# A transformer block's attention, re-cut into 32 units with the MLP's second product woven between their steps

## Chip, cores, metric

One core of a Trainium2 chip (trn2). The metric is the device time of one execution in microseconds. Executions of a kernel were timed in rounds beside executions of the kernel before, on the same chip.

Engines: PE (TensorE matmul), PEld (its weight load), DVE (VectorE), ACT (ScalarE), POOL (GpSimd). PSUM has 8 banks; a bank holds 128 x 512 fp32. "Granted clock" is the share of full speed that PE's throttle granted in the records; 1.00 is full speed.

## The reference, cut to what matters

```python
xn = layernorm(x)                       # x: 2048 tokens x 1024
out = x + A(xn) + B(xn)
# A: 32 heads of 32, four segments of 512 tokens, causal softmax inside a segment,
#    plus a linear memory M (phi(q) @ M / phi(q) @ z) carried over the segments; o = g*a_mem + (1-g)*a_dot; o @ wo
# B: h = layernorm(xn);  u = gelu(h^T w1 + b1) over tokens (F = 3584);  y = (u w2 + b2)^T
```

All large products come to 2816 matmuls of 128 x 128 x 512 in both kernels: 896 for each MLP product, 768 for q, k, v, 256 for `wo`. Attention itself is small on PE: per group of four heads 16 score matmuls, 40 for the weighted values, and a few for the memory.

## The kernel before

Five stages stand one after the other: layernorms; the first product; the second product with segment 0's projections between its tiles; four attention segments, with projections of the next segment and output projection of the last one as filler; a tail.

```python
def group_logits(self, s, i, g, step):          # LOGIT_STEPS = [[0], [1], [2, 3]]: blocks of 128 keys
    for r in range(4):                           # four heads, PSUM bank r each
        with fw.group(reads=[RkT[g], RqT[g]], writes=[self.R_bank[lb]]):
            for kb in kbs: fw.mm(...)            # scores, 32 rows of the array
        fw.op("act", ... activation(dst, ps_u, ACT.Exp, scale=SCALE) ...)      # one exp per head and step
        for kb in kbs: fw.op("pool", ... affine_select(diag, ...) ...)         # one causal mask per head and block
# ...
# gelu: Identity+bias on ACT, two scalar_tensor_tensor on DVE, Sigmoid on ACT, product on DVE
# output projection: its own accumulation, then
fw.op("dve", lambda e: e.tensor_tensor(dst, ps_t, dst, op=ALU.add), ...)       # onto rows read back from the output
```

Every operation goes through a helper that turns reads and writes into semaphore waits. One detail of it comes back later: a group of matmuls that writes a bank also waits for the last writer of that bank, even if that is PE itself.

```python
for r in writes:
    w = r.w                     # the token of the last writer, raised when its last matmul has completed
    ...
    add(w)
```

The softmax here doesn't subtract the row's maximum and nothing guards it: scores larger than these inputs give would overflow.

Of the kernel before, what the change touches and what calls it, by code (L numbers as in the profile page):

```python
# [23 lines left out]
C_GELU = 0.7978845608028654  # L24
K_CUBE = 0.044715
LN_EPS = 1e-5
MEM_EPS = 1e-6

PT_OFF = [0, 512, 896, 1152]
# [70 lines left out]
class FW:  # L100
    N_DMA_SEMS = 64
    N_OUT_SEMS = 24
# [161 lines left out]
class _BandStream:  # L264

    def __init__(self, fw, slots, slot_res, depth, issuer="sp"):
        self.fw = fw
        self.slots = slots
        self.res = slot_res
        self.n = len(slots)  # L270
        self.depth = depth
        self.bands = []
        self.issued = 0
        self.issuer = issuer

    def add(self, src_ap, dst_fn=None):
        self.bands.append((src_ap, dst_fn))
        return len(self.bands) - 1

    def slot_of(self, b):  # L280
        return b % self.n

    def ensure(self, b):
        target = min(b + self.depth, len(self.bands) - 1)
        while self.issued <= target:
            k = self.issued
            src, dst_fn = self.bands[k]
            si = self.slot_of(k)
            dst = dst_fn(self.slots[si]) if dst_fn else self.slots[si][:]
            self.fw.dma(dst, src, writes=[self.res[si]], issuer=self.issuer)  # L290
            self.issued += 1


class _Task:
    __slots__ = ("est", "run", "band")

    def __init__(self, est, run, band=None):
        self.est = est
        self.run = run
        self.band = band  # L300


class _Filler:
    def __init__(self, bands):
        self.q = deque()
        self.bands = bands
        self.budget = 0.0

    def add(self, tasks):
        self.q.extend(tasks)  # L310

    def total(self):
        return sum(t.est for t in self.q)

    def run_one(self):
        t = self.q.popleft()
        if t.band is not None:
            b, stream = t.band
            stream.ensure(b)
        t.run()  # L320
        return t.est

    def step(self, quantum):
        self.budget += quantum
        while self.q and self.budget >= self.q[0].est * 0.5 and self.budget > 0:
            self.budget -= self.run_one()

    def drain(self):
        while self.q:
            self.run_one()  # L330
        self.budget = 0.0
# [21 lines left out]
class _Kernel:  # L353
    def __init__(self, nc, ctx, A_x, A_wq, A_wk, A_wv, A_wo, A_beta, B_w1, B_b1, B_w2, B_b2, out):
        self.nc = nc
        self.ctx = ctx
        self.A_x, self.A_wq, self.A_wk, self.A_wv, self.A_wo, self.A_beta = A_x, A_wq, A_wk, A_wv, A_wo, A_beta
        self.B_w1, self.B_b1, self.B_w2, self.B_b2, self.out = B_w1, B_b1, B_w2, B_b2, out

    def sb(self, arena, shape, dtype, side):  # L360
        self._sb_n = getattr(self, "_sb_n", 0) + 1
        name = f"sbt{self._sb_n}"
        return arena.enter_context(self.nc.sbuf_tensor(name, list(shape), dtype, side=side))

    def res(self, name, init=None):
        return Res(name, init)

    def build(self):
        nc, ctx = self.nc, self.ctx
        fw = self.fw = FW(nc, ctx)  # L370

        self.x_d = self.A_x[0].rearrange("(c p) d -> p c d", p=P)
        self.out_d = self.out[0].rearrange("(c p) d -> p c d", p=P)

        self.ps = ctx.enter_context(nc.psum_tensor("ps_all", [P, 8, 512], F32))
        self.R_bank = [Res(f"bank{b}", bank=b) for b in range(8)]

        pa = self.pa = ExitStack()
        ctx.enter_context(pa)
        L = "left"  # L380
        self.ident = self.sb(pa, [P, P], BF16, L)
        self.brow1 = self.sb(pa, [N_FCH, P], BF16, L)
        self.brow2 = self.sb(pa, [N_TCH, P], BF16, L)
        self.beta_sb = self.sb(pa, [P, N_HEAD], BF16, L)
        self.gcol = self.sb(pa, [P, N_HEAD], F32, L)
        self.gm = self.sb(pa, [P, N_HEAD], F32, L)
        self.b1c = self.sb(pa, [P, N_FCH], F32, L)
        self.b2c = self.sb(pa, [P, N_TCH], F32, L)
        self.xnT = self.sb(pa, [P, N_DCH, S_TOK], BF16, L)
        LNR = self.LNR = 4  # L390
        self.ln_st = self.sb(pa, [P, 2, LNR, 12], F32, L)
        self.ln_mv = self.sb(pa, [P, 2, LNR, 2], F32, L)
        self.ln_rs = self.sb(pa, [P, 2, LNR], F32, L)
        self.ln_nb = self.sb(pa, [P, 2, LNR], F32, L)
        self.er = self.sb(pa, [P, 2, 512], BF16, L)
        self.MZ32 = self.sb(pa, [P, 8, 33], F32, L)
        self.MZbf = [self.sb(pa, [P, 8, 132], BF16, L) for _ in range(2)]
        self.s1 = self.sb(pa, [P, 4, 16], F32, L)
        self.s2 = self.sb(pa, [P, 4, 16], F32, L)

        self.R_ident = Res("ident")
        self.R_brow1 = Res("brow1")
        self.R_brow2 = Res("brow2")
        self.R_beta = Res("beta")
        self.R_gcol = Res("gcol")
        self.R_gm = Res("gm")
        self.R_b1c = Res("b1c")
        self.R_b2c = Res("b2c")
        self.R_xnT = [Res(f"xnT{c}") for c in range(N_TCH)]
        self.R_er = [Res(f"er{i}") for i in range(2)]  # L410
        self.R_MZ32 = [Res(f"mz32_{g}") for g in range(8)]
        self.R_MZbf = [[Res(f"mzbf{i}_{g}") for g in range(8)] for i in range(2)]
        self.R_lnA = [Res(f"lnA{c}") for c in range(LNR)]
        self.R_lnB = [Res(f"lnB{c}") for c in range(LNR)]
        self.R_s1 = Res("s1")
        self.R_s2 = Res("s2")
        self.R_out = [Res(f"outc{c}") for c in range(N_TCH)]

        bl = self.bl = ExitStack()
        Rt = "right"  # L420
        self.xB = self.sb(bl, [P, N_TCH, D_MODEL], BF16, Rt)
        self.gT = self.sb(bl, [P, N_FCH, D_MODEL], BF16, Rt)
        self.w2ring = [self.sb(bl, [P, N_FCH, P], BF16, Rt) for _ in range(2)]
        self.R_xB = [Res(f"xB{c}") for c in range(N_TCH)]
        self.R_gT = [[Res(f"gT{fc}_{h2}") for h2 in range(2)] for fc in range(N_FCH)]
        self.R_w2s = [Res(f"w2s{i}") for i in range(2)]

        be = self.be = ExitStack()
        self.h = self.sb(be, [P, N_TCH, D_MODEL], BF16, L)
        self.w1ring = [self.sb(be, [P, N_TCH, 256], BF16, L) for _ in range(2)]  # L430
        self.ga = [self.sb(be, [P, 512], F32, L) for _ in range(2)]
        self.ga2 = [self.sb(be, [P, 512], F32, L) for _ in range(2)]
        self.xn_tmp = [self.sb(be, [P, D_MODEL], BF16, L) for _ in range(2)]
        self.R_h = [Res(f"h{c}") for c in range(N_TCH)]
        self.R_w1s = [Res(f"w1s{i}") for i in range(2)]
        self.R_ga = [Res(f"ga{i}") for i in range(2)]
        self.R_ga2 = [Res(f"ga2_{i}") for i in range(2)]
        self.R_xnt = [Res(f"xnt{i}") for i in range(2)]

        self.qT = [None, None]  # L440
        self.kT = [None, None]
        self.pqT = [None, None]
        self.pk = [None, None]
        self.vA = [None, None]
        self.R_qT = [None, None]
        self.R_kT = [None, None]
        self.R_pqT = [None, None]
        self.R_pk = [None, None]
        self.R_vA = [None, None]

        block = ctx.enter_context(nc.Block())

        @block.sync
        def _(sp_eng):
            self.phase_prep()
            self.phase_B1()
            snap1 = fw.snapshot()
            self.be.close()
            self.alloc_A0(snap1)
            self.phase_B2_and_proj0()  # L460
            snap2 = fw.snapshot()
            self.bl.close()
            self.alloc_A_rest(snap2)
            self.phase_A()
            fw.final_waits()

    def alloc_A0(self, snap):
        a0 = self.a0 = ExitStack()
        self.ctx.enter_context(a0)
        L = "left"  # L470
        self.qT[0] = self.sb(a0, [P, 8, SEG_L], BF16, L)
        self.kT[0] = self.sb(a0, [P, 8, SEG_L], BF16, L)
        self.pqT[0] = self.sb(a0, [P, 8, SEG_L], BF16, L)
        self.pk[0] = self.sb(a0, [P, 4, D_MODEL], BF16, L)
        self.vA[0] = self.sb(a0, [P, 4, N_HEAD, 33], BF16, L)
        self.bands = [self.sb(a0, [P, N_DCH, 512], BF16, L) for _ in range(3)]
        self.R_qT[0] = [Res(f"qT0_{g}", snap) for g in range(8)]
        self.R_kT[0] = [Res(f"kT0_{g}", snap) for g in range(8)]
        self.R_pqT[0] = [Res(f"pqT0_{g}", snap) for g in range(8)]
        self.R_pk[0] = [[Res(f"pk0_{c}_{hh}", snap) for hh in range(2)] for c in range(4)]  # L480
# [655 lines left out]
```

## Time and profile before

| stage of the trace before | us | PE busy | granted clock |
|---|---|---|---|
| layernorms, with 4 banks of early first product | 65.3 | 31.2 | 0.88 |
| first product | 182.7 | 182.7 | 1.00 |
| second product, projections of segment 0 | 247.0 | 239.3 | 0.99 |
| attention, four segments | 390.0 | 318.4 | 0.88 |
| tail (last output projection) | 23.8 | 17.7 | 0.86 |

Median 909.7 us (907.9 to 912.1, 4 runs). The table is the view of windows, one window a stage. Its columns are: the window, its length, busy us (and instructions) of each engine, the granted clock, DMA share, GB/s.

```profile
65.30:248.00 182.70, 182.69 (x849) 82.94 (x846) 112.91 (x165) 73.16 (x112) 1.63 (x2) 1.00 0.31 80
495.00:885.00 390.00, 318.40 (x3260) 161.13 (x3260) 263.87 (x683) 203.72 (x452) 158.36 (x513) 0.88 0.26 87
```

The first page's busy line and two of its strips, each slice a fortieth of the span:

```profile
PE 789.3 (87%) x5506; PEld 377.3 (42%) x5506; DVE 494.6 (54%) x1123; ACT 318.2 (35%) x645; POOL 205.7 (23%) x555
...
PE   2479999999989999999997888798886979858867
...
PEclk9969999999999999999998988989998999976978
```

PE is 87% busy, but the strip shows where it isn't: in the first three slices and from the 22nd on, and there the clock falls too. What PE waited for in attention (view of waits, PE only, 495 to 885 us; total, times, longest):

```profile
PE ps_all L186 <- DVE sbt L1073: 18.2, 8, 2.7
PE ps_all L186 <- DVE sbt L867: 17.7, 10, 3.2
PE ps_all L192 <- DVE sbt L1106: 12.3, 3, 4.2
PE ps_all L186 <- ACT sbt L1017: 11.1, 30, 2.4
```

The waits are of several kinds: casts of the results (L1073), v casts (L867), the combine (L1106), exps (L1017). Dense work runs at one matmul of 128x512 in 215.8 ns, by the chain of waits (start, length, what):

```profile
379.22 13.81 PE ps_all L186 x64
```

### The profile page before, as it was taken

The numbers are of one execution on the slowest core, as the hardware profiler recorded it, in microseconds if no ns is written. First come the engines' busy times: TensorE is split into PE (matmuls) and PEld (weight loads), VectorE is DVE, ScalarE is ACT, GpSimd is POOL, SyncE is SP. The second block draws the span as 40 slices with busy tenths as digits, with TensorE's granted clock in tenths as the row PEclk, the third lists the DMA queues.
The fourth block names the chain that finished last, engine by engine and source line by source line (L and its number), as shares of the span: only waits on it lengthen the run. The fifth ranks groups of instructions, "written<-read, shape, count | busy, mean of one in ns | idle before, by whom it ended". The sixth has DMA issues, their size and how long they took to land.

```text
span 908.8 us, 14149 instructions
## 1 busy us (share of the span) xinstructions
PE 789.3 (87%) x5506; PEld 377.3 (42%) x5506; DVE 494.6 (54%) x1123; ACT 318.2 (35%) x645; POOL 205.7 (23%) x555
## 2 busy tenths in 40 slices
PE   2479999999989999999997888798886979858867
PEld 1234444444434444444442344444443434434434
DVE  6976765666622232222210576867677676675763
ACT  3335434333310000001100545654354544546730
POOL 4660000000010000000002334432332423426730
PEclk9969999999999999999998988989998999976978
DMA  8003223224364444525344221214232132510121
GB/s 278 1 1 93 79 61 93 67 74 112 61 182 108 110 93 101 103 53 105 65 92 138 70 94 49 93 48 139 92 106 83 57 130 94 186 48 2 48 93 47
DMA packets 128699, 80.62 MB, mean 89 GB/s; under 512 B 59002, under 2 KB 120442, under 8 KB 128634
## 3 DMA queue, kind: packets, MB, share of 16 engines
q1 hardware_dynamic: 122394, 73.43, 29.6%
q10 hardware_dynamic: 6240, 6.29, 2.2%
q8 instruction: 45, 0.74, 0.3%
q14 instruction: 20, 0.16, 0.1%
HBM read 71.32 MB, written 8.39 MB: 88 GB/s over the span
## 4 chain that ended last, share of the span: by engine, by line
PE 71%; DVE 20%; ACT 4%; DMA 2%; issue 2%; POOL 0%; SPq 0%; ACTq 0%; POOLq 0%
PE ps_all L186 70%; ACT sbt L1017 2%; DVE sbt L1067 2%; DVE sbt L1073 2%; DVE sbt L1104 1%; PE ps_all L192 1%; DVE sbt L1102 1%; DVE sbt L614 1%; DMA sbt<-in_A_wq_dram 1%; DVE sbt L613 1%; DVE sbt L849 1%; DVE sbt L646 1%; DVE sbt L1106 1%; DVE sbt L867 1%; ACT sbt L812 1%
## 5 line engine op out<-in xcount | busy, mean ns | idle before, releaser
L186 PE MATMUL ps_all<-sbt 128*128 128x512 bf16 (+5 forms) x5120 | 760.7, 312 | 74.9 <-DVE sbt L1073 18.2
L186 PEld LDWEIGHTS ps_all<-sbt 128*128 128x128 bf16 (+2 forms) x5120 | 349.4, 99 | 467.0 <-issue 94.3
L1017 ACT ACTIVATE sbt<-ps_all 128x384 bf16<-128x384 f32 (+1 forms) x384 | 169.6, 541 | 160.5 <-PE ps_all L186 122.1
L1021 POOL TENSOR_SCALAR_AFFINE_SELECT sbt<-sbt 128x128 bf16<-128x128 bf16 x512 | 156.9, 333 | 221.6 <-ACT sbt L1017 216.8
L751 DVE SCALAR_TENSOR_TENSOR sbt<-ps_all,sbt 128x512 bf16<-128x512 f32 x32 | 24.0, 751 | 150.3 <-PE ps_all L186 150.3
L192 PE MATMUL ps_all<-sbt 128*128 128x128 bf16 (+1 forms) x386 | 39.8, 255 | 39.2 <-POOL sbt L640 19.3
L712 ACT ACTIVATE sbt<-sbt 128x512 f32<-128x512 f32 x56 | 35.2, 629 | 82.2 <-DVE sbt L709 82.2
L812 ACT ACTIVATE sbt<-ps_all 128x512 bf16<-128x512 f32 x32 | 19.1, 598 | 119.7 <-DVE sbt L809 116.2
L715 DVE TENSOR_TENSOR sbt<-sbt 128x512 bf16<-128x512 f32 x56 | 38.8, 693 | 38.9 <-ACT sbt L712 38.9
L847 ACT ACTIVATE sbt<-ps_all 128x512 bf16<-128x512 bf16 x32 | 19.5, 610 | 112.8 <-PE ps_all L192 112.7
L1073 DVE CAST sbt<-ps_all 128x264 bf16<-128x264 f32 x128 | 53.6, 426 | 8.2 <-PE ps_all L186 7.1
L939 POOL MEMSET sbt<- 128x4224 bf16 x1 | 3.6, 3618 | 237.6 <-DMA out_dram<-sbt 237.6
L706 DVE SCALAR_TENSOR_TENSOR sbt<-sbt 128x512 f32<-128x512 f32 x56 | 38.7, 691 | 31.1 <-ACT sbt L703 31.1
L192 PEld LDWEIGHTS ps_all<-sbt 128*128 128x128 bf16 (+1 forms) x386 | 29.6, 115 | 58.5 <-POOL sbt L640 26.6
L703 ACT ACTIVATE sbt<-ps_all,sbt 128x512 f32<-128x512 f32 x56 | 38.2, 683 | 27.9 <-PE ps_all L186 27.9
L720 POOL MEMSET sbt<- 128x4224 bf16 x1 | 3.6, 3619 | 184.8 <-DVE sbt L715 184.8
L709 DVE SCALAR_TENSOR_TENSOR sbt<-sbt 128x512 f32<-128x512 f32 x56 | 38.8, 692 | 1.9
L828 DVE CAST sbt<-ps_all 128x512 bf16<-128x512 f32 x32 | 21.9, 689 | 32.1 <-PE ps_all L186 32.1
L809 DVE CAST sbt<-ps_all 128x512 bf16<-128x512 f32 x32 | 22.0, 687 | 29.8 <-PE ps_all L186 29.8
L904 DVE TENSOR_TENSOR sbt<-ps_all,sbt 128x512 bf16<-128x512 f32 x32 | 22.0, 689 | 26.9 <-PE ps_all L186 26.9
L867 DVE CAST sbt<-ps_all 128x512 bf16<-128x512 f32 x32 | 22.1, 690 | 22.0 <-PE ps_all L186 22.0
L849 DVE SCALAR_TENSOR_TENSOR sbt<-sbt 128x512 bf16<-128x512 bf16 x32 | 22.3, 696 | 21.4 <-ACT sbt L848 21.4
(47 smaller groups left out, 305.9 us busy)
## 6 DMA issues: line engine op xcount, KB each, us to landing
sbt<-in_B_w_dram SPq DMA_DIRECT2D x14, 1024.0 KB, 5.7
sbt<-in_B_w_dram SPq DMA_DIRECT2D x16, 896.0 KB, 6.5
sbt<-in_A_wo_dram SPq DMA_DIRECT2D x8, 1024.0 KB, 5.0
sbt<-in_A_wq_dram SPq DMA_DIRECT2D x6, 1024.0 KB, 5.4
sbt<-in_A_wk_dram SPq DMA_DIRECT2D x6, 1024.0 KB, 4.9
sbt<-in_A_wv_dram SPq DMA_DIRECT2D x6, 1024.0 KB, 4.9
sbt<-in_A_x_dram SPq DMA_DIRECT2D x4, 1024.0 KB, 8.9
out_dram<-sbt SPq DMA_DIRECT2D x16, 256.0 KB, 2.8
```

The costliest lines, as they stand in the source:

```text
L186: ins = self.nc.tensor.matmul(*args, **kwargs)
L192: ins = self.nc.tensor.transpose(out, in_, ident)
L703: fw.op("act", lambda e: e.activation(ga[:], ps_t, ACT.Identity, bias=self.b1c[:, fc:fc + 1], scale=1.0), reads=[self.R_bank[b], self.R_b1 ...
L706: fw.op("dve", lambda e: e.scalar_tensor_tensor(ga2[:], ga[:], K_CUBE, ga[:], op0=ALU.mult, op1=ALU.mult), reads=[Rga], writes=[Rga2])
L709: fw.op("dve", lambda e: e.scalar_tensor_tensor(ga2[:], ga2[:], 1.0, ga[:], op0=ALU.add, op1=ALU.mult), reads=[Rga2, Rga], writes=[Rga2])
L712: fw.op("act", lambda e: e.activation(ga2[:], ga2[:], ACT.Sigmoid, scale=2.0 * C_GELU), reads=[Rga2], writes=[Rga2])
L715: fw.op("dve", lambda e: e.tensor_tensor(dst, ga[:], ga2[:], op=ALU.mult), reads=[Rga, Rga2], writes=[self.R_gT[fc][half]])
L849: fw.op("dve", lambda e: e.scalar_tensor_tensor(dstk, e_ap, 1.0, dstk, op0=ALU.min, op1=ALU.add), reads=[Re, Rpk[c][hh]], writes=[Rpk[c][hh]])
L867: fw.op("dve", lambda e: e.tensor_copy(dst, ps_t.rearrange("p (hh d) -> p hh d", hh=16)), reads=[self.R_bank[bk]], writes=[RvA[c]])
L1017: fw.op("act", lambda e: e.activation(dst, ps_u, ACT.Exp, scale=SCALE), reads=[self.R_bank[lb]], writes=wr)
L1021: fw.op("pool", lambda e: e.affine_select(diag, diag, pattern=[[1, P]], compare_op=ALU.is_ge, fill=0.0, base=0, channel_multiplier=-1), re ...
L1073: fw.op("dve", lambda e: e.tensor_copy(dst, src), reads=small["pv"] + extra_reads, writes=[self.R_ost[gi][qb]])
```

## The change

The intent is to leave PE no gap. Attention is cut into 32 units (segment x group of four heads). A unit holds its three score steps, its four weighted sums, the projections of q and k for two units ahead, a quarter of a v block, and dense filler: 28 matmuls of the second product, and from segment 1 on 8 more of the output projection, so 36. Most of the filler stands right behind each of the three score steps, the rest at the unit's end. The output projection of segments 0 to 2 continues the second product's accumulation. Exp and mask work on four heads at once. GELU is one activation. The two layernorms are done from one set of statistics (the second variance follows from the first), and three first-product blocks, not two, are accumulated during them.

```diff
-        for r in range(4):
-            with fw.group(reads=[RkT[g], RqT[g]], writes=[self.R_bank[lb]]):
...
+        with fw.group(reads=[self.R_kT[k], self.R_qT[k]], writes=self.R_bank[0:4]):
+            for kb in kbs:
+                for r in range(4): fw.mm(...)
+        fw.op("act", lambda e: e.activation(self.pT[:, :, off:off + total], self.ps[:, 0:4, 0:total],
+                                            ACT.Exp, scale=SCALE), ...)
... (unit schedule)
+        for u in range(N_UNIT):
+            n = 28 if s == 0 else 36
+            n0, n1, n2 = (10, 8, 6) if s == 0 else (11, 9, 9)
+            n3 = n - n0 - n1 - n2
+            self.logits(u, 0)
+            if u: self.combine(u - 1)
+            self.main_emit(n0)
+            self.logits(u, 1)
+            self.main_emit(n1)
+            self.logits(u, 2)
+            self.main_emit(n2)
+            self.weigh(u, 0); self.weigh(u, 1)
+            self.proj_q(u + 2, 0)
+            self.o_transpose(u - 1, 2); self.k_transpose(u + 1, 3)
+            self.weigh(u, 2)
+            self.proj_k(u + 2, 1)
+            self.weigh(u, 3)
+            self.proj_v(m, u % 4, 2)
+            self.main_emit(n3)
... (the second product, joined with the output projection)
+            if at < N_FCH:
+                w, R_w = self.w2_ring.get(2 * j + at // 14)
+                end = min(at + n, (at // 14 + 1) * 14)
+            else:
+                end = min(at + n, total)                       # total = 28 + 8 where joined
+            with fw.group(reads=reads, writes=[self.R_bank[b]]):
+                for x in range(at, end):
+                    st, sp = x == 0, x == total - 1
+                    ...                                        # w2 x gT for x < 28, then oT x wo
... (gelu)
+        fw.op("act", ... activation(self.gT[...], self.bank(b), ACT.Gelu_apprx_tanh, bias=self.b1c[:, fc:fc + 1]), ...)
... (layernorm, pairs of chunks: rs = sqrt(1/(v + eps)) and sqrt(1/((1 + eps) v + eps^2)) in one square root)
+        fw.op("dve", lambda e: e.tensor_scalar(rs[:, :, 1:2], var, 1.0 + LN_EPS, LN_EPS * LN_EPS, ...))
```

## The prediction

> **What bounds the kernel now.** TensorE (PE), with four kinds of gap. The page gives PE 87% of 908.8 us; the windows split it:
>
> - Prologue (layernorms), 0 to 65 us: PE busy 27. VectorE is the bound (13.86 of every 15 us; 3.55 us per 128 tokens).
> - MLP first product, 66 to 248: dense. The chain shows 64 matmuls of 128x512 in 13.81 us, 215.8 ns each, which agrees with the Trainium skill, "TensorE: Matmul & The Clock Gate", section "Wait — 56ns, not 53.3ns?" (215.7 warm).
> - Second product and first projections, 248 to 495: dense but for a few us (an A_wq load, 5.4, on the chain).
> - Attention, 495 to 885 = 390 us. PE busy about 318. PE's waits are on DVE and ACT: 18.2 us on the 128x264 casts, 17.7 on v casts, 12.3 on the combine, 11.1 on exp. The same page (HAM clock gate) ties a low clock to idle; the trace agrees: 1.00 in dense windows, 0.80 where PE was busy 62%.
> - Tail, 885 to 909: 24 us.
>
> **PE work stays.** 2816 matmuls of 128x512 in both. The memory update's 384 become 96 wider; 32 memory reads and 32 transposes go.
>
> **What moves.** 896 second-product matmuls go under attention; the output projection of 12 of 16 chunks joins their accumulation, so 24 DVE adds and the read-back vanish. Exps over four heads: 3 instructions a group, not 12 (604 and 510 ns now; from that slope I estimate 1.8, 1.4, 1.4 us), masks 4, not 16.
>
> **Sum, after.**
> - Prologue: DVE per pair of chunks: 4 bn_stats at 0.72, 2 aggregates at 0.24, small operations 0.8, one normalisation 0.5: 4.7 us, against 7.1. 8 pairs after a first load at 3.5, plus pipeline: dense PE from about 47. 6 banks of hidden work are then done, not 4.
> - Hidden: 50 tiles x 16 x 0.2158 = 173, to 220.
> - First v, q, k: 64 x 0.2158 = 14, plus 3 of bubble: 237.
> - Units: attention's own PE work costs 2.9 us a group where the trace is dense (751.1 to 762.8: 11.73 us hold 40 of 128x512, 8.63, and one group). Transposes 0.45. Segment 0: 52 x 0.2158 + 3.1 = 14.3. Segments 1, 2: 60 x 0.2158 + 3.4 = 16.3. Segment 3: 15.9 less missing projections. Total 115 + 262 + 113 = 490 if dense. ACT needs 7 us a unit, DVE 9, POOL 3. The slack between score steps is thin (11 matmuls = 2.4 us against an exp of 1.8 plus latencies), so I add 0.55 a unit: 508, to 745.
> - Tail: 56 matmuls, transpose, 8 DVE adds at 0.72, last store 2.8: 22, to 767.
>
> Critical path: prologue -19, two tiles -7, joint at 248 -3, attention with second product about -112 (waits filled, clock kept at 1.00).
>
> **Predicted: 767 us, 8 in 10 between 748 and 790.** Faster 0.97, same 0.02, slower 0.01.
>
> **To check.** PE busy 95% or more after the prologue; granted clock 0.98 or more in the units; units of 14.5 to 15 us in segment 0, 16.5 to 17 in 1 and 2; dense PE from 44 to 51 us; tail 20 to 24.
>
> **What would make it wrong.** Wide exps or masks slower than their slopes say; a late buffer release in each unit (banks 0 to 3 serve scores and projections), times 32; POOL and DVE delaying each other in the prologue (a 128x1 DVE multiply takes 737 ns there against 206); a late second w1 load.

## The result

758.1 us median (757.7 to 758.7, 4 runs) against 909.7. The ratio is 0.833 (95% interval 0.831 to 0.835). Here and below a ratio is the mean time of one kernel's fast runs over that of the other's fast runs of the same rounds, so not quite the ratio of the medians.

The page after, the lines that answer to those above:

```profile
PE 717.7 (95%) x5058; PEld 338.3 (45%) x5154; DVE 277.2 (37%) x617; ACT 280.4 (37%) x301; POOL 112.3 (15%) x154
...
PE   0999999999998999999999999999999999999996
...
PEclk9999999999999999999999999999999999999999
```

The strip is full from the second slice on, but for one slice of 8 tenths and the last, and the clock stays in its top tenth. By stages (windows, columns as above): norms, first product, first projections, units of segment 0, 1, 2, 3, tail:

```profile
0.00:50.90 50.90, 31.46 (x222) 17.71 (x227) 35.00 (x97) 28.38 (x35) 25.42 (x26) 1.00 0.51 145
50.90:223.75 172.85, 172.01 (x786) 78.34 (x801) 0.00 (x0) 38.54 (x57) 0.00 (x0) 1.00 0.37 94
223.75:239.70 15.95, 14.15 (x69) 6.46 (x69) 5.15 (x8) 3.76 (x5) 0.00 (x0) 1.00 0.85 241
239.70:354.00 114.30, 112.50 (x935) 54.09 (x952) 42.77 (x110) 51.30 (x49) 19.92 (x32) 1.00 0.35 74
354.00:485.00 131.00, 128.20 (x1030) 60.88 (x1049) 65.55 (x141) 54.74 (x56) 22.11 (x32) 1.00 0.37 77
485.00:616.00 131.00, 128.23 (x1010) 60.37 (x1028) 66.78 (x142) 54.25 (x55) 22.43 (x32) 1.00 0.37 77
616.00:736.00 120.00, 116.92 (x949) 54.10 (x966) 54.06 (x109) 48.87 (x44) 22.42 (x32) 1.00 0.29 61
736.00:756.90 20.90, 14.27 (x68) 6.35 (x67) 7.93 (x14) 0.60 (x1) 0.00 (x0) 0.95 0.32 114
```

| | before | after | difference | predicted |
|---|---|---|---|---|
| norms, to dense PE | 65.3 | 50.9 | -14.4 | -19 (to about 47) |
| first product after that | 182.7 | 172.9 | -9.8 | -7 |
| second product, projections, attention | 637.0 | 512.3 | -124.7 | -115 (3 joint + 112) |
| tail | 23.8 | 20.9 | -2.9 | -2 |

The windows also split the 124.7 us of the third row. PE stood idle for 79.3 of the 637.0 us before and for 12.3 of 512.3 after, 67 less; it was busy for 557.7 us before and 500.0 after, 58 less. The 58 go with the higher clock and with the small matmuls that were dropped; no run here divides them.

What PE waited for over the whole trace after, the first four entries:

```profile
PE ps_all L194 <- DMA brow_50<-in_B_b_dram: 15.2, 1, 15.2
PE ps_all L188 <- issue: 2.2, 1, 2.2
PE ps_all L188 <- PE ps_all L188: 2.2, 14, 0.2
PE ps_all L188 <- DVE pk_1733 L673: 1.7, 1, 1.7
```

Nothing of attention is left among the waits except 1.7 us at its very start, in 239 to 736 us. What remains is the load of a bias row at the start (15.2 us; in e12_norm below, where PE does not wait for it, PE's first work still comes only at 12.9 us, after the first layernorm) and an odd entry: PE waiting for PE. It lists only 14 short waits; the experiments will show that there were more.

### The profile page after: what moved, and what is told of

Read it like the earlier page. It is cut to its first block, busy times and chain, and to the rows that moved or that the text cites. A ratio compares the mean times of both kernels' runs of the same rounds, so it can differ in the third digit from the quotient of the medians.

```text
span 756.9 us, 11693 instructions
## 1 busy us (share of the span) xinstructions
PE 717.7 (95%) x5058; PEld 338.3 (45%) x5154; DVE 277.2 (37%) x617; ACT 280.4 (37%) x301; POOL 112.3 (15%) x154
## 4 chain that ended last, share of the span: by engine, by line
PE 92%; DVE 4%; issue 2%; SPq 1%; DMA 1%; ACT 0%; DVEq 0%; another core or an unknown queue 0%
PE ps_all L188 90%; PE ps_all L194 2%; DVE ln_st L575 1%; SPq L210 1%; DVE ln_st L574 1%; DMA brow_51<-in_B_b_dram 1%; DVE ln_mv L576 0%; DVE xn_tmp_76 L607 0%; DVE ln_rs L584 0%; DVE fin_8202 L966 0%; DVE fin_8203 L966 0%; ACT xn_tmp_75 L604 0%; DVE xn_tmp_74 L607 0%; DVE ln_rs L585 0%; ACT xnT_70 L622 0%
## 5 line engine op out<-in xcount | busy, mean ns | idle before, releaser
L743 ACT ACTIVATE pT<-ps_all 128x1536 bf16<-128x1536 f32 (+1 forms) x96 | 152.9, 1593 | 201.6 <-PE ps_all L188 201.6
L749 POOL TENSOR_SCALAR_AFFINE_SELECT pT<-pT 128x512 bf16<-128x512 bf16 x128 | 86.9, 691 | 599.5 <-ACT pT L743 599.5
L662 ACT ACTIVATE gT<-ps_all,b1c 128x512 bf16<-128x512 f32 x56 | 37.8, 689 | 134.5 <-PE ps_all L188 134.5
L710 DVE CAST vA_63<-ps_all 128x512 bf16<-128x512 f32 x16 | 11.1, 694 | 187.9 <-PE ps_all L188 187.7
L188 PE MATMUL ps_all<-h,w1s_79 128*128 128x512 bf16 x311 | 72.9, 385 | 2.7 <-issue 2.2
L188 PE MATMUL ps_all<-h,w1s_80 128*128 128x512 bf16 x314 | 72.4, 381 | 0.3
L188 PE MATMUL ps_all<-h,w1s_81 128*128 128x512 bf16 x251 | 55.6, 379 | 0.3
L188 PE MATMUL ps_all<-gT,w2h_671 128*128 128x512 bf16 x213 | 53.0, 380 | 2.8 <-PE ps_all L188 0.9
L188 PE MATMUL ps_all<-gT,w2h_673 128*128 128x512 bf16 x214 | 53.1, 380 | 2.6 <-PE ps_all L188 1.1
L188 PE MATMUL ps_all<-gT,w2h_670 128*128 128x512 bf16 x219 | 53.6, 381 | 0.3
L188 PE MATMUL ps_all<-gT,w2h_672 128*128 128x512 bf16 x218 | 53.3, 381 | 0.4 <-PE ps_all L188 0.2
L783 DVE CAST ost_1736<-ps_all 128x264 bf16<-128x264 f32 (+1 forms) x64 | 23.7, 391 | 79.6 <-PE ps_all L188 79.6
L783 DVE CAST ost_1737<-ps_all 128x264 bf16<-128x264 f32 (+1 forms) x64 | 23.7, 392 | 74.7 <-PE ps_all L188 74.7
L188 PEld LDWEIGHTS ps_all<-h,w1s_80 128*128 128x128 bf16 x320 | 31.5, 98 | 38.4 <-issue 1.1
L188 PEld LDWEIGHTS ps_all<-h,w1s_79 128*128 128x128 bf16 x320 | 30.9, 99 | 37.1 <-issue 3.6
L188 PEld LDWEIGHTS ps_all<-h,w1s_81 128*128 128x128 bf16 x256 | 25.0, 98 | 30.2
L188 PE MATMUL ps_all<-wo_sb,oT_1744 128*128 128x512 bf16 x126 | 32.6, 380 | 1.4 <-remote 0.3
L188 PEld LDWEIGHTS ps_all<-gT,w2h_671 128*128 128x128 bf16 x224 | 19.4, 97 | 30.8 <-PE ps_all L188 6.9
L188 PEld LDWEIGHTS ps_all<-gT,w2h_673 128*128 128x128 bf16 x224 | 19.4, 97 | 30.8 <-PE ps_all L188 6.9
L188 PE MATMUL ps_all<-wo_sb,xnT_68 128*128 128x512 bf16 x127 | 30.6, 380 | 1.2 <-ACT xnT_68 L835 0.7
L188 PEld LDWEIGHTS ps_all<-gT,w2h_672 128*128 128x128 bf16 x224 | 19.3, 98 | 25.3 <-issue 3.6
L188 PEld LDWEIGHTS ps_all<-gT,w2h_670 128*128 128x128 bf16 x224 | 19.3, 98 | 25.3 <-issue 3.6
```

What stands on the lines that cost most here:

```text
L188: ins = self.nc.tensor.matmul(*args, **kwargs)
L662: fw.op("act", lambda e: e.activation(self.gT[:, fc, half * 512:(half + 1) * 512], self.bank(b), ACT.Gelu_apprx_tanh, bias=self.b1c[:, fc: ...
L710: fw.op("dve", lambda e: e.tensor_copy(self.vA[i][:, c, :, 0:D_HEAD], self.bank(b).rearrange("p (h d) -> p h d", d=D_HEAD)), reads=[self.R ...
L743: fw.op("act", lambda e: e.activation(self.pT[:, :, off:off + total], self.ps[:, 0:4, 0:total], ACT.Exp, scale=SCALE), reads=self.R_bank[0:4],
L749: fw.op("pool", lambda e: e.affine_select(d, d, pattern=[[0, 4], [1, P]], compare_op=ALU.is_ge, fill=0.0, base=0, channel_multiplier=-1), ...
L783: fw.op("dve", lambda e: e.tensor_copy(dst, self.ps[:, b, 0:n * VW]), reads=[self.R_bank[b]], writes=[self.R_ost[o][qb]])
```

## The experiments

Theory A: the gain in the 637 us is the dense work standing between a unit's dependent steps; it fills the waits and so also holds the clock up. Rival B: the gain is the leaner attention, with fewer and wider operations on ACT, DVE and POOL. Rival C: the placement inside a unit does not matter, only that each unit carries dense work. The kernel before also had filler between its score steps (projections), so A is about more of it and about its places.

### The second product in four lumps (e1_lumped)

```diff
-            n0, n1, n2 = (10, 8, 6) if s == 0 else (11, 9, 9)
-            n3 = n - n0 - n1 - n2
+            n0 = n1 = n2 = 0
+            n3 = 288 if u in (8, 16, 24) else 0        # and 224 ahead of unit 0
```

> The changed kernel with every instruction kept, but the second product (and its joined output projection) issued in four lumps, one a segment, between units and not inside them. Theory A (the gain is the dense work standing between the score steps): PE waits about 2.1, 1.4 and 1.0 us for the three exps in each unit and about 0.9 for the v cast at its end, so about 5.4 us x 32 units, 758 + 173 = 930 us (890 to 980), PE clock below 0.95 in the units, lumps dense. Rival B (the gain is the leaner attention: 3 exps for 12, 4 masks for 16, fewer small VectorE operations): below 800 us.

Measured: 1009.5 us (median of the three fast executions), ratio to before 1.109 (1.106 to 1.112), granted clock 0.865 to 0.867 over the fast executions. B falls as a cause that would do alone: with all of its lean operations the kernel is 11% slower than the one before. The loss is larger than A's range. The profiled execution was a slow one (2054.6 us, told at the end), so its trace is not read for the reason; the next run has a clean one.

### The same filler at each unit's end (e2_unit_end)

```diff
-            n0, n1, n2 = (10, 8, 6) if s == 0 else (11, 9, 9)
-            n3 = n - n0 - n1 - n2
+            n0 = n1 = n2 = 0
+            n3 = n
```

> The changed kernel, each unit keeping its 28 or 36 matmuls of the second product, but all at the unit's end and none between the score steps. Theory A: PE waits about 2.1 + 1.4 + 1.0 = 4.5 us a unit for the exps, 758 + 144 = 900 us (860 to 930); the clock stays nearer 1.00 than in the lumped run since each unit has 13 us of dense work. Rival B: below 800. Rival C (what matters is only that every unit has enough dense work to keep the clock up): within 2% of 758.

Measured: 984.1 us, ratio to before 1.081 (1.078 to 1.085). C falls as well: same units, same instructions, only the places differ, and the time is 226 us longer, beyond A's range of 860 to 930 too. PE's wait for exps in the whole trace, and then, from the timeline, a part of one unit on PE (start, length, what, count; in brackets the idle time before it and its releaser):

```profile
PE ps_all L188 <- ACT pT L743: 150.6, 94, 2.0
```

```profile
557.77 0.34 PE L188 MATMUL ps_all<-qT,kT 32*128 32x384 bf16 x4 [1.99 <-ACT pT L743]
559.67 0.34 PE L188 MATMUL ps_all<-qT,kT 32*128 32x256 bf16 x8 [1.56 <-ACT pT L743]
...
562.04 3.19 PE L188 MATMUL ps_all<-xnT,wq 128*128 128x512 bf16 x7 [1.15 <-ACT pT L743]
```

The three waits for exp are 1.99, 1.56 and 1.15 us, together 4.7, where 4.5 was expected; over all units 150.6 us. The rest, 226 - 151 = 75 us, is what the expectation missed. It lies in PE's busy time: 794.9 us in this trace and 717.7 in the changed kernel's, 77 more for the same instructions. The q projection after the waits, 8 matmuls of which the trace has 7, takes 3.19 us, where 8 such matmuls take 1.89 in the changed kernel. The windows of segments 0 to 2 say why:

```profile
240.17:411.70 171.53, 130.60 (x940) 62.12 (x956) 45.35 (x113) 51.33 (x49) 19.97 (x32) 0.82 0.22 50
411.70:603.63 191.93, 151.71 (x1040) 71.95 (x1056) 68.79 (x143) 54.76 (x57) 22.12 (x32) 0.85 0.23 53
603.63:794.56 190.93, 150.92 (x1036) 71.37 (x1052) 69.40 (x143) 54.27 (x56) 22.43 (x32) 0.86 0.24 53
```

The clock is 0.82 to 0.86 although no gap of PE in the units is longer than 2.0 us and each unit has more than 10 us of dense work. The Trainium skill, "TensorE: Matmul & The Clock Gate", section "HAM oscillation — how this bites in real kernels", gives gaps over about 3.4 us as what to avoid. Its next section, "A second HAM failure mode: psum-queue depth-cycling", names shorter idles, without a length. Here three gaps of 1.2 to 2.0 us in each unit of 23.9 us were enough. They lie close together, though: from 555.40 to 562.04 PE was busy for only 1.85 of 6.64 us. Whether single gaps or this sparse stretch lowered the clock is not shown.

### The wide exps and masks alone, in the kernel before (e3_before_wide)

```diff
-        for r in range(4): ... group on bank r, exp of head r, masks of head r
+        with fw.group(reads=[RkT[g], RqT[g]], writes=self.R_bank[0:4]): ... four heads
+        fw.op("act", lambda e: e.activation(pT2[:, :, off:off + total], self.ps[:, 0:4, 0:total], ACT.Exp, ...))
+        for kb in kbs: one affine_select over [[0, 4], [1, P]]
```

> The kernel before with one part of the change alone: one exp over four heads (3 a group, not 12) and one mask over four heads (4, not 16). Theory A: PE waited 11.1 us for exps in all, ACT was busy 204 of 390 us in attention: 909 falls by 0 to 30 us, to 880 to 909. Rival B: it falls by 60 us or more, below 850.

Measured: 922.0 us, ratio 1.013 (1.010 to 1.015): 1.3% slower. It lies outside both expectations. Its waits in attention, the first two:

```profile
PE ps_all L186 <- ACT sbt L1013: 33.2, 25, 3.5
PE ps_all L186 <- DVE sbt L868: 20.1, 10, 3.6
```

PE's wait for exps rose from 11.1 to 33.2 us. One exp over four banks gives none of them back until it has read all, so the next step's first score cannot start early. The two timelines show it, first the kernel before, then this run (exps and the next step's scores):

```profile
840.24 5.13 ACT L1017 ACTIVATE sbt<-ps_all 128x512 bf16<-128x512 f32 x12 [1.94 <-PE ps_all L186]
840.98 0.32 PE L186 MATMUL ps_all<-sbt 32*128 32x384 bf16 x1 [0.51 <-ACT sbt L1017]
```

```profile
855.49 1.88 ACT L1013 ACTIVATE sbt<-ps_all 128x2048 bf16<-128x2048 f32 x1 [3.04 <-PE ps_all L186]
857.51 0.34 PE L186 MATMUL ps_all<-sbt 32*128 32x384 bf16 x4 [1.79 <-ACT sbt L1013]
```

The first score starts 0.74 us after the first narrow exp began, and 2.02 us after the wide one began. ACT was less busy (188 of 405 us in attention, 204 of 390 before) and PE waited longer.

### The narrow exps and masks in the changed kernel (e4_narrow)

```diff
-        fw.op("act", ... activation(self.pT[:, :, off:off + total], self.ps[:, 0:4, 0:total], ...))
+        for r in range(4): fw.op("act", ... activation(self.pT[:, r, off:off + total], self.ps[:, r, 0:total], ...))
```
(the masks per head as well)

> The changed kernel with the 12 exps and 16 masks a group of before. ACT needs about 1.7 us more a unit (8.7 of about 16). Theory A: the dense matmuls between the steps hide nearly all of it, 0 to 0.4 us a unit: 758 to 771. Rival B: 40 us slower or more, above 798.

Measured: 758.0 us, beside 758.1 with the wide ones. Between dense matmuls neither form costs anything, so the wider exps and masks are no part of the gain in this schedule.

### The five-operation GELU (e5_gelu5)

```diff
-            ACT.Gelu_apprx_tanh from PSUM to gT
+            Identity + bias (ACT), two scalar_tensor_tensor (DVE), Sigmoid (ACT), product (DVE)
```

> The changed kernel with the five-operation GELU of before (2 ACT, 3 VectorE; one shared intermediate tile for room). Theory A: a tile's chain of about 2.9 us stands beside 3.45 us of matmuls and the first projections cover the last one: 757 to 762. Rival B (relief of VectorE and ACT counts everywhere): 10 us slower or more.

Measured: 758.6 us. Off the critical path, as expected.

### The output projection in its own accumulation (e6_unfused)

```diff
-                self.main.append((n, c, half, c < 12))
+                self.main.append((n, c, half, 0))
+                if c < 12:
+                    self.main.append((n, c, half, 1))      # 8 matmuls, the other bank, then a DVE add
```

> The changed kernel with the output projection of segments 0 to 2 in its own accumulation again: 24 more VectorE adds of 0.69 us, same matmuls at the same places in the units. Theory A: VectorE is busy about half of a unit, PE need not wait: 757 to 762. Rival B: 24 x 0.69 = 17 us slower.

Measured: 753.4 us (753.0 to 753.5), that is 4.7 us faster: joining the projection to the accumulation costs time. (e5_gelu5, in the same rounds, took 758.6 us, so the chip is not the reason.) Neither expectation had this. The unit of segments 1 and 2 takes 16.34 us here and 16.58 in the changed kernel (the start of the first exp, over 15 units). The place shows on PE. In the changed kernel, between two score steps and after the last:

```profile
408.24 0.82 PE L188 MATMUL ps_all<-gT,w2h_672 128*128 128x512 bf16 x3
409.12 1.47 PE L188 MATMUL ps_all<-gT,w2h_673 128*128 128x512 bf16 x6
410.52 0.34 PE L188 MATMUL ps_all<-qT_1726,kT_1729 32*128 32x256 bf16 x8
410.80 1.90 PE L188 MATMUL ps_all<-gT,w2h_673 128*128 128x512 bf16 x8
412.76 0.39 PE L188 MATMUL ps_all<-wo_sb,oT_1744 128*128 128x512 bf16 x1
```

Three matmuls from 408.24 at 0.2158 us each end at 408.89, yet the next starts at 409.12. Eight from 410.80 end at 412.53, yet the first `wo` matmul starts at 412.76. Both are joints inside one bank: the other half of the weights' buffer, then `wo`. There a new group begins, and the helper makes it wait for the last group in that bank, hence for PE's own pipeline. Matmuls of 128x512 start 0.216 us apart but take 0.380 us each in the trace, so I estimate that waiting for one to complete costs at least the difference, 0.164. The Trainium skill, "TensorE: Matmul & The Clock Gate", section "Single matmul latency", gives (398 + N)/2.4 ns warm, 379 ns for N = 512; this trace agrees with 380, but the profile models the ends of matmuls, so this is no independent check. In the unjoined kernel the projection goes to the other bank and only the first joint is left. This was an argument from two traces, so it was tested below.

### The old layernorm order (e7_old_ln)

```diff
-            ln_stats x2, ln_small (one square root for both norms), ln_bias, ln_apply (DVE and ACT in turn)
+            ln_d1, ln_a1, ln_d2, ln_a2x, ln_d3, ln_p1 of the kernel before, both copies on POOL
```

> The changed kernel with the layernorm arithmetic and order of before (two square roots one after the other, both normalised copies on GpSimd), three early hidden blocks kept. Theory A: VectorE takes 3.55 us a chunk again, dense PE starts at about 65 us, not 51: 758 + 14 = 772 (767 to 778).

Measured: 776.7 us, 18.6 more; dense PE starts at 68 us. A little more than expected, in the direction expected: three early blocks were kept, and PE waited 18.2 us for POOL's copies.

### Two early blocks (e9_early2)

```diff
-    N_EARLY = 3
+    N_EARLY = 2
```

> The changed kernel with two early hidden blocks (4 banks) in the norm stage as before, not three. If VectorE bounds that stage, the third block is free and the loss is two tiles, 6.9 us: 765. If PE bounds it (as the trace after suggests from 34 us on, 1.74 us of PE a chunk), the stage shortens by up to 16 x 0.43 and the loss is smaller: 758 to 763.

Measured: 764.3 us, 6.2 more. PE's wait for ACT's copies of the transposes grew from 1.6 to 9.6 us: without the third block PE mostly idles. The stage's last transposes come only 0.8 us sooner (48.53 us, 49.35 in the changed kernel), so PE hardly bounds the stage, and the third block is nearly free.

### Small repairs at both ends of attention (e8_tail), and in the norms (e10_all)

```diff
-        self.k_transpose(0, 0)
+        self.k_transpose(0, 5)
-        tail: 7 of 8 blocks with 7 matmuls each (49), last o_transpose, the 8th block, then the 8 last matmuls, each with its add
+        tail: 3 blocks of 7, last o_transpose, 1 of 7, their 4 last matmuls with adds, then 4 whole blocks with adds
```

> The changed kernel with two small repairs: the first transpose of k in a bank that the first scores do not use (1.74 us of PE wait in the trace), and in the tail the last transpose of the attention output after 21 matmuls and not after 49, so that finished blocks are added and stored while PE still works (I estimate 3 to 4 us). Expected 758 - 5 = 753 (751 to 756).

Measured: 753.1 us (751.5 to 753.6), as expected.

```diff
+            ln_stats(2p); ln_bias and ln_apply of the last pair; ln_stats(2p + 1); ln_small
+            bias transposes after the last pair; third early block from chunk 4 on
+            load of x chunks 2 and 3 ahead of that of beta
```

> As e8_tail, and in the norm stage: the bias transposes at the stage's end (PE and VectorE waited there until 15.2 us for their load), the third early hidden block joined from the fourth chunk on (its weights land last), the normalisation of a pair issued between the two statistics of the next. If the stage is bound by VectorE, 2 to 4 us less than e8_tail: 750 (747 to 753).

Measured: 754.6 us, no better than e8_tail; the repair failed. In its trace an operation of two elements stands while POOL works (POOL and DVE, start, length):

```profile
31.15 2.64 POOL L610 TENSOR_SCALAR h<-xin,ln_rs,ln_nb 128x1024 bf16<-128x1024 bf16 x2 [2.12 <-DVE ln_nb L595]
...
33.24 0.57 DVE L585 TENSOR_SCALAR ln_rs<-ln_mv 128x2 f32<-128x2 f32 x1
```

It ends at 33.81, POOL at 33.79. In the changed kernel the same operation falls after POOL's pair and takes 0.17 us:

```profile
33.14 2.64 POOL L609 TENSOR_SCALAR h<-xin,ln_rs,ln_nb 128x1024 bf16<-128x1024 bf16 x2 [1.71 <-DVE ln_nb L594]
...
36.77 0.17 DVE L584 TENSOR_SCALAR ln_rs<-ln_mv 128x2 f32<-128x2 f32 x1
```

The new order put it under POOL in seven of the eight pairs, about 0.40 us each. That this is what spoiled the repair fits the trace, but no run changed it alone. The Trainium skill, "GPSIMD Engine Reference", section "Specifications", says POOL shares its SBUF interfaces with VectorE and contends with some of its operations; both traces agree, and so does the kernel before, where one multiply of 128x1 stood until POOL's operation ended and took 737 ns, and its twin after it 206.

### One group for one run of matmuls (e11_one_group), and the norms once more (e12_norm)

```diff
-                end = min(at + n, (at // 14 + 1) * 14)
-                reads = [R_w] + ...
+            end = min(at + n, total)
+            W = {q: self.w2_ring.get(2 * j + q) for q in sorted({x // 14 for x in range(at, end) if x < N_FCH})}
+            reads = every weight half, gT block and oT block that the run needs
             with fw.group(reads=reads, writes=[self.R_bank[b]]):
```

On top of e8_tail. The wait is not taken out; the group boundary that made it is gone.

> e8_tail, with the joined projection kept, but the matmuls that one call issues into one accumulation recorded as one group, also across the joint of the two halves of the second product's weights and the joint with the output projection. In the traces PE stands about 0.23 us at each such joint inside a run of matmuls into one bank (two joints a unit in segments 1 to 3, one in segment 0), and the kernel without the joined projection, which has only the first kind, was 4.7 us faster. Theory D (a group waits for the one before it in the same bank to leave the array): (24 x 2 + 8) x 0.23 = 13 us less than e8_tail, 740 (737 to 745), units of 16.1 us in segments 1 and 2. Rival E (the other weights or the other buffers slow the joined matmuls): no change, 753.

Measured: 738.6 us (738.3 to 739.0), ratio to before 0.811 (0.809 to 0.813), 14.5 us less than e8_tail. Units of segments 1 and 2 take 16.06 us (16.58 before this), those of segment 0 14.16 (14.43): 0.26 us a joint. The same place as above:

```profile
404.63 1.90 PE L188 MATMUL ps_all<-gT,w2h 128*128 128x512 bf16 x8
406.36 0.38 PE L188 MATMUL ps_all<-wo_sb,oT 128*128 128x512 bf16 x1
```

Eight matmuls from 404.63 end at 406.36, and `wo` starts at 406.36. The entry "PE waiting for PE" is gone from the view of waits. D holds, E falls: the joined projection is harmless once it is no new group. (The view had listed 14 waits of 2.2 us in all, not 56 of 14.5: it reckons from the modelled ends of matmuls, so it shows only part of each hole.) This is the fastest version.

> e11_one_group, and the norm stage with the constants, the gate's sigmoid and the bias transposes moved behind it and the third early hidden block joined from the fourth chunk on; VectorE's order as in the changed kernel (the run with a new order lost 0.4 us a pair to an operation that stood while GpSimd ran). VectorE loses 1.1 us of waiting and 1.3 us of small operations, PE pays about 0.6 us for the transposes: 2 us less than e11_one_group (0 to 4).

Measured: 739.8 us, 1.2 more than e11_one_group. The early hidden work did start sooner, but the bias copies now stood on DVE behind an operation that waited for the late sigmoid and its table load on ACT, and PE waited for them:

```profile
PE ps_all L188 <- DVE b2c L546: 1.8, 1, 1.8
```

My arrangement spoiled it. What the norm stage could still give stays open.

## Why the prediction was right, point by point

- **Time.** 767 was said, with 748 to 790; 758.1 came.
- **Where the gain lies.** Right: -125 of -152 us in attention with the second product. e1 and e2 show that the new cut needs the placement: 226 us hang on where 28 or 36 matmuls stand in a unit. Of these about 151 are waits for exp and 75 the lower clock with what else runs slower after a gap. They do not apportion the 125 us: in the kernel before, PE's waits in attention were mostly for DVE (53.5 of 71.6 us; 11.1 for exps). Whether the filler alone removed those, or the leaner DVE work (263.9 us busy in the four segments before, 229.2 in the 32 units after) had a part, is not shown; no run gave the changed kernel the old casts and combine.
- **"ACT needs 7 us a unit, DVE 9, POOL 3."** None binds, as said. In the trace after, ACT is busy 54.7 of 131 us in segment 1 (6.8 a unit), DVE 65.6 (8.2), POOL 22.1 (2.8). The exps measured 1.88 and 1.45 us, estimated 1.8 and 1.4. Making them wide was not worth anything (e4), and alone it hurts (e3); the prediction did not claim a figure for it.
- **"so I add 0.55 a unit".** The cause was wrong, and that the size nearly fits is luck. The term was 18 us for thin slack between score steps, but not one wait for exp appears in the units. What was there instead are waits of PE for itself at joints of groups, 14.5 us in all (e11), 0.27 to 0.52 a unit. The "490 if dense" was right within 2%: 496.3 measured, less 14.5 of joints, leaves 482. So the sum for the units was 12 us too high, which more than made up for the late start (next but one).
- **"the output projection ... joins their accumulation, so 24 DVE adds and the read-back vanish".** True but worth nothing, and as built it cost 4.7 us (e6).
- **"dense PE from about 47".** 50.9. DVE's pair took 4.36 us, less than the 4.7 of the sum, but the sum had x always there after its first load. The trace has DVE idle for 1.8 us before the second pair's load landed; then DVE did constants and waited 0.9 us in all for PE's transposes of the bias rows, which came at 15.16. Its third pair began at 15.93, where 3.45 + 2 x 4.36 gives 12.2. In e12_norm, without the constants and bias rows there, it stood for x until 14.7 us all the same, so most of this 3.7 us is the arrival of x. The faster pairs won back 2.7: DVE's eighth pair ended at about 42.3, and the sum has 41.1. The other 2.7 of the 3.9 us lie behind it, in the "pipeline" term: 8.6 us from there to dense PE, where the sum left 5.9. (The prediction's "PE busy 27" in 0 to 65 us was a slip; the windows give 30.9.)
- **Checks.** After the norms PE was busy 686 of 706 us, 97% (95 or more said); clock 1.00 (0.98); units 14.45 in segment 0 (14.5 to 15, just missed) and 16.58 in 1 and 2 (16.5 to 17); tail 20.9 (20 to 24).

## What to carry to other kernels

When a short chain of dependent steps runs on PE, dense work is worth most between the steps, in pieces about as long as the wait to be covered (their lengths were not varied here); in e2_unit_end the same work after the chain filled none of the waits, and the slower running that came with the gaps cost half as much again as the gaps (75 beside 151 us). Judge a fusion or a wider instruction by what it holds: one exp over four banks holds four banks. When PE is 95% busy, lay the starts of consecutive matmuls beside their dense interval: a hole of 0.23 us inside one accumulation was a wait that the helper had made, and 56 of them were 2% of the kernel.

## What the Trainium skill lacked or had wrong

- "TensorE: Matmul & The Clock Gate", section "HAM oscillation — how this bites in real kernels", warns of PE gaps over about 3.4 us, and the section after it of short idles without a length. In e2_unit_end the longest wait of PE in the units was 2.0 us, three waits of 4.7 us together in each 23.9 (inside a stretch of 6.64 us with PE busy for 1.85), and the granted clock was 0.82 to 0.86.
- No page that I read gives the cost of a PE group waiting for PE's own last matmul in the same bank. It was 0.26 us at N = 512 (14.5 us over 56 joints).
- One execution of e1_lumped took 2054.6 us, three others 1008 to 1010. Its trace has a mean duration of about 830 ns for matmuls of 128x512 all through, with a recorded granted clock of 1.00. "TensorE: Matmul & The Clock Gate", section "Seeing it yourself", warns that clock events in traces can be unreliable, but has no case like this, with the recorded clock at full through a whole slow run; the cause is open.
